# A decode forward-and-backward kernel: ten resident weight chunks, 1 MB zero stores issued by GpSimd alone, and a VectorE share in the w1 backward

## The chip, the cores and the metric

The kernel runs on one core of one Trainium2 chip. The metric is the time of one execution on the device in microseconds (us). Most executions of one kernel agree within a few tenths of a per cent, but different chips differ by more, so every kernel is compared with runs of the kernel before on the same chip. Runs are labelled fast or slow by their time and their clock.

Engines in the profile: PE is TensorE, PEld its weight loads, DVE is VectorE, ACT is ScalarE, POOL is GpSimd, SP is SyncE. A trailing q (SPq, POOLq) is the engine's instruction queue. "L138" is a line of the kernel. GB/s is what the 16 DMA engines moved.

## The reference, cut to what matters

One token (1,024 numbers) goes through attention A, an MLP B, the same A again and the same B again, each with a layer norm and a residual. Then all gradients are formed.

```python
    # D = 1024, 32 heads of 128, 4 groups of keys and values, F = 3584, Sk = 32768, W = 4096
    def _A_ref(x, k_cache, v_cache, wq, wo):
        q = (x @ wq).reshape(...)
        k = jnp.repeat(k_cache[:, :, Sk - W:, :], rep, axis=1)   # only the last 4,096 keys
        v = jnp.repeat(v_cache[:, :, Sk - W:, :], rep, axis=1)
        ...
        return softmax(q k * Dh ** -0.5) v @ wo
    def _B_ref(x, w1, b1, w2):
        h = x @ w1 + b1
        return mish(h) @ w2
    x = x + _A_ref(_layernorm(x), k_cache, v_cache, wq, wo)      # A1
    x = x + _B_ref(_layernorm(x), w1, b1, w2)                    # B2
    x = x + _A_ref(_layernorm(x), k_cache, v_cache, wq, wo)      # A3
    x = x + _B_ref(_layernorm(x), w1, b1, w2)                    # B4
    # outputs: x and the gradients of x, k_cache, v_cache, wq, wo, w1, b1, w2
```

The gradients of k_cache and v_cache have the shape of the whole caches. Outside the window of 4,096 keys they are zero, and these zeros have to be written: 2 caches x 4 groups x 28,672 x 128 numbers of 2 bytes, 58.7 MB. That is a third of all bytes this kernel moves. The zeros depend on nothing, so they can be stored at any time: they are the filling with which the DMA can be kept busy while TensorE works through a chain.

## The kernel before

The order of the stages is A1, B2, A3 and B4 forward (B4 fused with its backward), then A3 backward, the w2 pass and the w1 backward of B2, A1 backward, and last the "end": outer products of columns and rows, which are the weight gradients, copied from PSUM to SBUF and stored. The weight wo is cut in 16 chunks of 0.5 MB; nine stay resident in SBUF (`NR = 9`), the others go through six stream buffers (`NB = 6`) each time they are needed, as do w1 and w2.

The zeros come from a tile of 4 KB per partition, in 112 stores of 0.5 MB. GpSimd issues 76 of them in the background, behind a copy (`gate_t`) that waits for a value of the stage; SyncE issues the remaining 36 in A1 backward, as soon as its last weight loads are out.

```python
    ZC = 2048
    zt = keep.tile([P, ZC], BF16, name="zt")
    nc.gpsimd.memset(zt[:], 0.0)
    # ... cut: zero_jobs is the list of 112 pieces [P, ZC] of the two outputs
    def zeros(n):
        for _ in range(min(n, len(zero_jobs))):
            nc.sync.dma_start(zero_jobs.pop(0), zt[:])
    gate_t = keep.tile([P, 1], BF16, name="gate_t")
    def bg_zeros(n, after):
        if n:
            nc.gpsimd.tensor_copy(gate_t[:], after[:, 0:1])
        for _ in range(min(n, len(zero_jobs))):
            nc.gpsimd.dma_start(zero_jobs.pop(0), zt[:])
    # ... cut
    Z = dict(B2=3, A3=16, B4=[5, 2, 1, 2, 1, 2, 6], A3c=6, A3d=26, W1=3, A1c=3, A1d=36)
```

Z says how many stores each stage issues: B2, A3 and B4 forward, A3c and A3d in A3 backward, W1 in the w1 backward, A1c and A1d in A1 backward.

The w1 backward streams 16 half rows of w1. T loads one and transposes its 14 blocks of 128x128 (the matvec here needs w1 with the other axis on the partitions); M multiplies a half row with the gradient of the hidden layer.

```python
        def T(i):
            w = w1_load(i)
            ws[i] = w
            xpose(*alt_blocks(w[:, 0:1024], 4))
            xpose(*alt_blocks(w[:, 1024:1792], 3))
        def M(i, _):
            w, t, hf = ws.pop(i), i // 2, i % 2
            for b in range(NW2):
                fb = hf * NW2 + b
                mv(nacc, t, w[:, b * P:(b + 1) * P], sv["dh_bf"][:, fb:fb + 1], i == 0 and b == 0, fb == TF - 1)
        level()
        bg_zeros(Z["W1"], sv["dh_bf"])
        pipe(list(range(2 * TD)), T, M)
        return ln_bwd(nacc.cols(0, TD), sv["n32"], sv["rstd"], g_col, lname, nxt)
```

## Time and profile before

The kernel takes 451.71 us (median of 3 runs, 450.68 to 451.8). The profiled execution took 456.97 us and is labelled slow.

From the page of the kernel before: the span, the busy share of the DMA engines (tenths, 40 equal slices of 11.4 us), what they moved, the packets, and the queue that GpSimd fills.

```profile
span 454.9 us, 11941 instructions
DMA  8999997999999978999999799999999999999994
GB/s 323 385 412 422 407 409 281 381 322 370 417 416 384 404 238 282 354 392 411 419 413 414 273 362 349 321 400 417 415 417 420 418 416 417 419 418 419 419 420 172
DMA packets 52257, 172.25 MB, mean 379 GB/s; under 512 B 5200, under 2 KB 12396, under 8 KB 51180
q0 software_dynamic: 11040, 39.86, 22.0%
```

Where nothing holds the DMA back it moves 415 to 420 GB/s. At 418 GB/s the 172.25 MB take 412 us, so only 43 us of the span are DMA time not used. This gives a measure for each stage, called "lost": the stage's length minus its bytes divided by 418 GB/s. From about 300 us to the end almost nothing is lost: there the kernel is bound by DMA. The dips lie earlier.

The TensorE timeline of the kernel before shows the waits that the change aims at (start, busy us, instruction, and in brackets the idle time before it and what ended it):

```profile
140.31 0.56 PE L229 MATMUL sm<-o_pair,wo_c 128*128 128x16 bf16 x16 [3.62 <-DMA wo_c<-in_A_wo_dram]
162.84 0.60 PE L229 MATMUL sm<-nB_pair,w_b 128*128 128x16 bf16 x16 [4.50 <-DMA w_b<-in_B_w_dram]
210.23 1.03 PE L193 MATMUL tps<-ident_bf,wo_c 128*128 128x128 bf16 x8 [2.65 <-DMA wo_c<-in_A_wo_dram]
```

The seventh chunk of wo has to wait until one of six buffers is free.

### The profile page before, as it was taken

The page shows a single profiled execution, that of the slowest core. Times are in us where ns is not written, and L with a number is a line of the kernel's source. Part 1 is how long each engine was busy: PE and PEld are TensorE (multiplying, and loading weights), DVE is VectorE, ACT ScalarE, POOL GpSimd, SP SyncE. Part 2 cuts the span into 40 slices and gives each one's busy share as a digit, 9 for nine tenths or more (in the row PEclk, how much of TensorE's full clock was granted, in tenths as well). Part 3 has the DMA queues.
Part 4 walks back from the last instruction along what each step waited for, and adds up shares of the span by engine and source line. Part 5 has one row for each costly group of instructions (what it writes and reads, how often), then busy time and mean ns, then how long its engine had stood idle before and what let it go on. Part 6 is the DMA issues. An engine that isn't in the chain of part 4 may idle for free.

```text
span 454.9 us, 11941 instructions
## 1 busy us (share of the span) xinstructions
PE 324.7 (71%) x5107; PEld 224.4 (49%) x5107; DVE 236.6 (52%) x489; ACT 225.2 (50%) x262; POOL 56.6 (12%) x146
## 2 busy tenths in 40 slices
PE   0566854497896968985999888977868679897300
PEld 0334524387566968974687888844631111121000
DVE  3124101197422736683344874572359889999400
ACT  1122100075332837777365553536329899989400
POOL 2000000001422111341242002042010000000000
PEclk9997565578967969997879557999975555555555
DMA  8999997999999978999999799999999999999994
GB/s 323 385 412 422 407 409 281 381 322 370 417 416 384 404 238 282 354 392 411 419 413 414 273 362 349 321 400 417 415 417 420 418 416 417 419 418 419 419 420 172
DMA packets 52257, 172.25 MB, mean 379 GB/s; under 512 B 5200, under 2 KB 12396, under 8 KB 51180
## 3 DMA queue, kind: packets, MB, share of 16 engines
q1 hardware_dynamic: 41120, 131.61, 74.5%
q0 software_dynamic: 11040, 39.86, 22.0%
q8 instruction: 40, 0.66, 0.5%
q14 instruction: 13, 0.11, 0.1%
q10 hardware_dynamic: 44, 0.01, 0.0%
HBM read 72.89 MB, written 98.58 MB: 377 GB/s over the span
## 4 chain that ended last, share of the span: by engine, by line
PE 21%; ACT 12%; DMA 7%; issue 4%; SPq 3%; DVE 3%; DVEq 0%; POOL 0%; ACTq 0%; POOLq 0%
PE ops L229 7%; PE tps L193 7%; ACT wq_b L148 6%; DMA w_c<-in_B_w_dram 4%; PE acc L229 3%; SPq L129 3%; DMA wo_c<-in_A_wo_dram 2%; ACT st_o L148 2%; DMA out_dram<-zt 1%; ACT wo_b L148 1%; ACT K L148 1%; ACT V L148 1%; PE d L229 1%; PE tps L623 1%; ACT wo_c L148 1%
## 5 line engine op out<-in xcount | busy, mean ns | idle before, releaser
L138 POOL DMA_DIRECT2D out_dram<-zt x76 | 40.4, 536 | 44.5 <-DMA out_dram<-zt 41.9
L229 PEld LDWEIGHTS <-w_c 128*128 128x128 bf16 x1120 | 37.3, 103 | 16.7 <-DMA w_c<-in_B_w_dram 13.4
L633 ACT COPY w_c<-tps 128x1024 bf16<-128x1024 bf16 x28 | 28.2, 1012 | 21.7 <-PE tps L623 11.8
L229 PE MATMUL ops<-V 2*128 2x512 bf16 (+1 forms) x160 | 34.8, 598 | 5.9 <-ACT wq_b L148 3.4
L647 DVE CUSTOM_DVE_ANT_0 scr<-w_c,gbc 128x1024 bf16<-128x1024 bf16 x28 | 34.2, 1220 | 4.3 <-DMA w_c<-in_B_w_dram 2.2
L145 DVE CAST wq_b<-ops 128x1024 bf16<-128x1024 f32 (+1 forms) x31 | 33.8, 1148 | 3.8 <-PE ops L229 3.2
L148 ACT CAST wq_b<-ops 128x1024 bf16<-128x1024 f32 (+1 forms) x33 | 33.7, 1140 | 2.2 <-PE ops L229 2.0
L148 ACT COPY K<-tps 128x1024 bf16<-128x1024 bf16 x19 | 18.7, 1029 | 30.2 <-PE tps L193 30.2
L229 PE MATMUL ops<-wo_b 2*128 2x512 bf16 x120 | 23.3, 567 | 10.9 <-ACT wq_b L148 7.2
L229 PEld LDWEIGHTS <-V 128*128 128x128 bf16 (+2 forms) x416 | 14.2, 102 | 27.8 <-issue 27.6
L623 PE MATMUL tps<-ident_bf,w_c 128*128 128x128 bf16 x224 | 24.5, 276 | 1.1 <-DMA w_c<-in_B_w_dram 0.7
L148 ACT COPY w_b<-tps 128x1024 bf16<-128x1024 bf16 x20 | 19.5, 1015 | 6.7 <-PE tps L193 6.7
L145 DVE COPY K<-tps 128x1024 bf16<-128x1024 bf16 x13 | 8.9, 690 | 25.8 <-PE tps L193 25.8
L193 PE MATMUL tps<-ident_bf,K 128*128 128x128 bf16 x256 | 22.1, 252 | 0.1
L229 PE MATMUL q<-wq_b,nA_pair 128*32 128x512 bf16 x128 | 11.2, 440 | 15.0 <-DMA wq_b<-in_A_wq_dram 14.9
L193 PEld LDWEIGHTS <-K 128*128 128x128 bf16 x256 | 18.6, 115 | 4.5 <-issue 4.4
L813 DVE CUSTOM_DVE_ANT_0 wo_c<-wo_c,gbc 128x1024 bf16<-128x1024 bf16 x14 | 16.4, 1217 | 8.0 <-DMA wo_c<-in_A_wo_dram 4.3
L229 PEld LDWEIGHTS <-wo_b 2*128 2x128 bf16 (+1 forms) x152 | 5.6, 99 | 29.3 <-issue 28.6
L623 PEld LDWEIGHTS <-w_c 128*128 128x128 bf16 x224 | 18.5, 124 | 1.7 <-issue 0.9
L148 ACT CAST K<-ops 128x1024 bf16<-128x1024 f32 x18 | 17.7, 1014 | 2.5 <-PE ops L229 1.8
L193 PE MATMUL tps<-ident_bf,w_c 128*128 128x128 bf16 x224 | 17.1, 236 | 2.3 <-DMA w_c<-in_B_w_dram 2.3
L193 PE MATMUL tps<-ident_bf,wq_b 128*128 128x128 bf16 x256 | 18.0, 238 | 1.0 <-issue 1.0
(323 smaller groups left out, 651.9 us busy)
## 6 DMA issues: line engine op xcount, KB each, us to landing
out_dram<-zt POOLq DMA_DIRECT2D x76, 512.0 KB, 10.6
out_dram<-zt SPq DMA_DIRECT2D x36, 512.0 KB, 10.3
wo_c<-in_A_wo_dram SPq DMA_DIRECT2D x28, 512.0 KB, 8.4
w_c<-in_B_w_dram SPq DMA_DIRECT2D x32, 448.0 KB, 6.4
w_c<-in_B_w_dram SPq DMA_DIRECT2D x28, 512.0 KB, 6.0
out_dram<-wq_b SPq DMA_DIRECT2D x17, 512.0 KB, 11.4
wq_b<-in_A_wq_dram SPq DMA_DIRECT2D x16, 512.0 KB, 11.6
out_dram<-K SPq DMA_DIRECT2D x8, 1024.0 KB, 12.7
```

The source lines that it names most:

```text
L129: nc.sync.dma_start(zero_jobs.pop(0), zt[:])
L138: nc.gpsimd.dma_start(zero_jobs.pop(0), zt[:])
L145: nc.vector.tensor_copy(out_ap, in_ap)
L148: nc.scalar.copy(out_ap, in_ap)
L193: nc.tensor.transpose(ps[:, b, :], ap, ident_bf[:])
L229: nc.tensor.matmul(out_ap, lhsT=lhsT, rhs=rhs, start=start, stop=stop, skip_group_check=True, **kw)
L623: nc.tensor.transpose(self.ps[c][:, b, :], w[:, 1, b * P:(b + 1) * P], ident_bf[:])
L633: nc.scalar.copy(self.w[c][:, 1, :], self.ps.pop(c)[:].rearrange("p b c -> p (b c)"))
L647: nc.vector.tensor_tensor_reduce(out=scr[:], in0=w[:, 0, :], in1=gbc[:], scale=1.0, scalar=0.0, op0=ALU.mult, op1=ALU.add, accum_out=self. ...
L813: nc.vector.tensor_tensor_reduce(out=w[:, 0, :], in0=w[:, 0, :], in1=gbc[:], scale=1.0, scalar=0.0, op0=ALU.mult, op1=ALU.add, accum_out=w ...
```

## The change

Its intent: keep a tenth chunk of wo in SBUF, so that six late chunks meet six buffers; find the room for it by shrinking constants and by halving the tile of zeros (2 KB per partition, read four times for a store of 1 MB, with half as many instructions); let GpSimd issue all zeros and place them anew; and in the w1 backward let VectorE sum 1,024 of every 3,584 columns, with the matvecs two tiles behind the transposes. Small parts: warm-up matmuls in three gaps, a broadcast moved behind the first loads of B2, a row layout by four small matmuls.

```diff
-NR = 9
+NR = 10
...
-    ZC = 2048
-    zt = keep.tile([P, ZC], BF16, name="zt")
+    ZC = 4096
+    zt = keep.tile([P, ZC // 4], BF16, name="zt")
     nc.gpsimd.memset(zt[:], 0.0)
+    zt2 = zt[:, None, :].to_broadcast([P, 4, ZC // 4])
...
-    def zeros(n):
-        for _ in range(min(n, len(zero_jobs))):
-            nc.sync.dma_start(zero_jobs.pop(0), zt[:])
+                zero_jobs.append(zflat[:, i * ZC:(i + 1) * ZC].rearrange("p (a b) -> p a b", a=4))
...
-        if n:
+        if n and after is not None:
             nc.gpsimd.tensor_copy(gate_t[:], after[:, 0:1])
         for _ in range(min(n, len(zero_jobs))):
-            nc.gpsimd.dma_start(zero_jobs.pop(0), zt[:])
+            nc.gpsimd.dma_start(zero_jobs.pop(0), zt2)
... (mlp_fwd, B2)
-        gbc = bcast_row(g_bf)
+            if i == 4:
+                gbc = bcast_row(g_bf)
+                bg_zeros(Z["B2a"], n_bf)
... (w1 backward)
+        def V(i):
+            if i % 2 == 0:
+                wv = ws[i][:, 0:1024].rearrange("p (y t) -> p t y", t=2)
+                nc.vector.tensor_tensor_reduce(out=wv, in0=wv, in1=big[0][:].rearrange("p (t y) -> p t y", t=2), scale=1.0, scalar=0.0,
+                                               op0=ALU.mult, op1=ALU.add, accum_out=tw[:, i // 2:i // 2 + 1])
...
-        pipe(list(range(2 * TD)), T, M)
+        V(0)
+        for i in range(2, 2 * TD):
+            T(i)
+            V(i)
+            M(i - 2)
+        M(2 * TD - 2)
+        M(2 * TD - 1)
... (A1 backward)
             after_stream()
-            zeros(Z["A1d"])
...
             nextprep(2)
+            bg_zeros(Z["A1d"], None)
             warm(3)
...
             rows_put(area["Rq"], 1, "dq", "heads")
+            bg_zeros(Z["A1e"], None)
...
-    Z = dict(B2=3, A3=16, B4=[5, 2, 1, 2, 1, 2, 6], A3c=6, A3d=26, W1=3, A1c=3, A1d=36)
+    Z = dict(B2a=1, B2={NW2 - 2: 1}, A3=6, B4=[0, 1, 1, 1, 1, 1, 2], A3c=3, A3d=15, B4w={}, W1=0, A1c=6, A1d=5, A1e=100)
... (cut: onesD as a broadcast of one column, pat removed, row_layout and over_groups by tile_position, warm-up matmuls, order of late chunks)
```

In the new Z a unit is 1 MB. The last 12 stores (A1e) are issued by GpSimd behind `rows_put(... "dq" ...)`, a few copies on GpSimd that need the result of the attention backward (dq).

More of the change, by code (lines that the diff above doesn't have):

```diff
@@ L98 @@
     nc.scalar.dma_start(b_row, B_b1.rearrange("(c x) -> c x", x=2 * P))
-    onesD = keep.tile([P, P], FP32, name="onesD")
-    nc.vector.memset(onesD[:], invD)
+    ones1 = keep.tile([P, 1], FP32, name="ones1")
+    nc.vector.memset(ones1[:], invD)
+    onesD = ones1[:, 0:1].to_broadcast([P, P])
     eps_t = keep.tile([P, 1], FP32, name="eps_t")
@@ L124 @@
             for i in range(per // ZC):
-                zero_jobs.append(zflat[:, i * ZC:(i + 1) * ZC])
-    def zeros(n):
-        for _ in range(min(n, len(zero_jobs))):
-            nc.sync.dma_start(zero_jobs.pop(0), zt[:])
+                zero_jobs.append(zflat[:, i * ZC:(i + 1) * ZC].rearrange("p (a b) -> p a b", a=4))
     gate_t = keep.tile([P, 1], BF16, name="gate_t")
     def bg_zeros(n, after):
-        if n:
+        if n and after is not None:
             nc.gpsimd.tensor_copy(gate_t[:], after[:, 0:1])
         for _ in range(min(n, len(zero_jobs))):
-            nc.gpsimd.dma_start(zero_jobs.pop(0), zt[:])
+            nc.gpsimd.dma_start(zero_jobs.pop(0), zt2)
     ev = [0.0, 0.0]
@@ L261, in __call__, with over_groups @@
             return self.ap[:, j:j + 5:4]
+    def over_groups(out, rhs, start, stop):
+        for c in range(NC):
+            mm(out[32 * c:32 * c + 32, :], fold[:], rhs, start, stop, tile_position=(0, 32 * c))
     pre = []
@@ L281, in ln_fwd @@
         sps = sm_tile(P, 2 * TD)
-        nc.tensor.matmul(sps[:], lhsT=onesD[:], rhs=xx[:], start=True, stop=True)
+        nc.tensor.matmul(sps[:], lhsT=onesD, rhs=xx[:], start=True, stop=True)
         if name == "A3":
@@ L298, in ln_fwd, with ln_bwd @@
         return n32, n_bf, rstd
-    def ln_bwd(dn_ps, n32, rstd, g_col, name, nxt):
+    def ln_bwd(dn_ps, n32, rstd, g_col, name, nxt, more=None):
         tt = work.tile([P, 2 * TD], FP32, name="tt")
-        nc.vector.tensor_copy(tt[:, 0:TD], dn_ps)
+        if more is None:
+            nc.vector.tensor_copy(tt[:, 0:TD], dn_ps)
+        else:
+            nc.vector.tensor_add(tt[:, 0:TD], dn_ps, more)
         nc.vector.tensor_mul(tt[:, TD:], tt[:, 0:TD], n32[:])
         sps = sm_tile(P, 2 * TD)
-        nc.tensor.matmul(sps[:], lhsT=onesD[:], rhs=tt[:], start=True, stop=True)
+        nc.tensor.matmul(sps[:], lhsT=onesD, rhs=tt[:], start=True, stop=True)
         if nxt == "A1":
@@ L391, in row_layout @@
         x = area[name].rearrange("p (g d) -> p g d", g=G)
-        ps = psum1([P, P], BF16, "rps")
-        nc.tensor.transpose(ps[:, 0:P], col32[:], ident_bf[:])
+        ps = psum1([P, P], FP32, "rps")
+        for c in range(NC):
+            mm(ps[32 * c:32 * c + 32, 0:P], col32[:], ident_bf[:], True, True, tile_position=(0, 32 * c))
         for g in range(G):
@@ L404, in pad_cols @@
                              src_ps.rearrange("p (g h) -> p g h", g=G), ACT.Copy, scale=sc)
-        rep = keep.tile([P, NC, HQ], BF16, name=name + "_rep")
+        rep = keep.tile([P, HQ], BF16, name=name + "_rep")
         nc.vector.tensor_copy(
-            rep[:].rearrange("p c (g h) -> p c g h", g=G),
-            pad[:].rearrange("p (g x) -> p g x", x=40)[:, None, :, 0:8].to_broadcast([P, NC, G, 8]))
+            rep[:].rearrange("p (g h) -> p g h", g=G), pad[:].rearrange("p (g x) -> p g x", x=40)[:, :, 0:8])
         return rep
@@ L506, in attn_fwd @@
         sdg = work.tile([P, HQ], FP32, name="sdg", tag="u")
-        nc.vector.tensor_scalar(out=sdg[:, 0:32], in0=pat[:, 0, :], scalar1=ssum[:, 0:1], scalar2=None, op0=ALU.mult)
+        nc.vector.tensor_scalar(out=sdg[:, 0:32], in0=fold[:], scalar1=ssum[:, 0:1], scalar2=None, op0=ALU.mult)
         sps = sm_tile(P, HQ)
-        nc.tensor.matmul(sps[:, 0:32], lhsT=onesD[:], rhs=sdg[:, 0:32], start=True, stop=True)
+        nc.tensor.matmul(sps[:, 0:32], lhsT=onesD, rhs=sdg[:, 0:32], start=True, stop=True)
         rbc = work.tile([P, HQ], FP32, name="rbc", tag="r")
@@ L528, in attn_fwd @@
         lps = sm_tile(P, 1)
-        nc.tensor.matmul(lps[:], lhsT=pat[:].rearrange("p c x -> p (c x)"), rhs=ssum[:], start=True, stop=True)
+        over_groups(lps, ssum[:], True, True)
         lns = work.tile([P, 1], FP32, name="lns")
@@ L540, in attn_fwd @@
         late, early = list(range(NR, NO)), list(range(NR))
-        order = early + late if first else late[0:1] + early + late[1:]
+        order = early + late if first else late[0:3] + early + late[3:]
         for i, c in enumerate(order):
@@ L554, in attn_fwd @@
                 rows_sel2(yr, Cols8(yacc.cols(0, TD), False))
-            if not first and i == 0:
-                held[NO - 1] = wo_load(NO - 1)
             if not first:
@@ L650, in rest @@
                     self.bwd(c - 1, g_bf)
-                if c == NW2 - 2 and zn:
-                    bg_zeros(zn, self.wg[:, c, :])
+                if c in zn:
+                    bg_zeros(zn[c], self.wg[:, c, :])
             self.bwd(NW2 - 1, g_bf)
@@ L774, in mlp_bwd_w1, with blocks @@
         ws = {}
+        tw = work.tile([P, TD], FP32, name="tw", tag="xx", padded_shape=[P, 2 * TD])
+        big = []
+        def blocks(i):
+            return range(8 if i % 2 == 0 else 0, NW2)
         def T(i):
@@ L778, in T, with M @@
             ws[i] = w
-            xpose(*alt_blocks(w[:, 0:1024], 4))
+            if i % 2:
+                xpose(*alt_blocks(w[:, 0:1024], 4))
             xpose(*alt_blocks(w[:, 1024:1792], 3))
-        def M(i, _):
+        def M(i):
             w, t, hf = ws.pop(i), i // 2, i % 2
-            for b in range(NW2):
+            for b in blocks(i):
                 fb = hf * NW2 + b
-                mv(nacc, t, w[:, b * P:(b + 1) * P], sv["dh_bf"][:, fb:fb + 1], i == 0 and b == 0, fb == TF - 1)
+                mv(nacc, t, w[:, b * P:(b + 1) * P], sv["dh_bf"][:, fb:fb + 1], i == 0 and b == 8, fb == TF - 1)
+        def V(i):
+            if i % 2 == 0:
+                ev[0] += 1.3
+                wv = ws[i][:, 0:1024].rearrange("p (y t) -> p t y", t=2)
+                nc.vector.tensor_tensor_reduce(out=wv, in0=wv, in1=big[0][:].rearrange("p (t y) -> p t y", t=2), scale=1.0, scalar=0.0,
+                                               op0=ALU.mult, op1=ALU.add, accum_out=tw[:, i // 2:i // 2 + 1])
         level()
         bg_zeros(Z["W1"], sv["dh_bf"])
-        pipe(list(range(2 * TD)), T, M)
-        return ln_bwd(nacc.cols(0, TD), sv["n32"], sv["rstd"], g_col, lname, nxt)
+        rep8 = work.tile([P, TD, P], BF16, name="rep8", tag="kp")
+        nc.vector.tensor_copy(rep8[:], sv["dh_bf"][:, 0:TD, None].to_broadcast([P, TD, P]))
+        T(0)
+        T(1)
+        top("two")
+        big.append(pools["top"].tile([P, D], FP32, name="dhbc"))
+        for k in range(TD):
+            at = (k % 2) * 4 + k // 2
+            mm(big[0][:, at * P:(at + 1) * P], rep8[:, k, :], ident_bf[:], k < 2, True)
+        V(0)
[5 more added lines that the diff above has]
+        M(2 * TD - 1)
+        return ln_bwd(nacc.cols(0, TD), sv["n32"], sv["rstd"], g_col, lname, nxt, tw[:])
     def attn_bwd(g_col, g_bf, lname, sv, first, nxt):
@@ L829, in attn_bwd @@
         T(0)
-        bwd_rows2(dacc, wo_kept[NR - 1], NR - 1, g_bf, started=False)
+        for c in range(8, NR):
+            bwd_rows2(dacc, wo_kept[c], c, g_bf, started=c > 8)
         T(1)
@@ L845, in attn_bwd @@
                 lambda: rows_put(area["R1"], 1, "dh", "pieces"),
-                lambda: row_layout(sA3["dorep"][:].rearrange("p c x -> p (c x)"), "do3"),
-                lambda: row_layout(sA3["qrep"][:].rearrange("p c x -> p (c x)"), "q3"),
+                lambda: row_layout(sA3["dorep"], "do3"),
+                lambda: row_layout(sA3["qrep"], "q3"),
             ])
@@ L898, in attn_bwd @@
                 lambda: rows_put(area["Rq"], 0, "nA", "rep"),
-                lambda: row_layout(sA1["dorep"][:].rearrange("p c x -> p (c x)"), "do1"),
-                lambda: row_layout(sA1["qrep"][:].rearrange("p c x -> p (c x)"), "q1"),
+                lambda: row_layout(sA1["dorep"], "do1"),
+                lambda: row_layout(sA1["qrep"], "q1"),
                 db1_out,
@@ L912, in attn_bwd @@
         for hf in range(2):
-            nc.tensor.matmul(lps[:], lhsT=pat[:].rearrange("p c x -> p (c x)"), rhs=sdp[:, hf:hf + 1], start=hf == 0, stop=hf == 1)
+            over_groups(lps, sdp[:, hf:hf + 1], hf == 0, hf == 1)
         sd = work.tile([P, 1], FP32, name="sd")
@@ L957, in col_out @@
     def col_out(cols, n, out_flat):
-        ps = psum1([2 * HQ, P], BF16, "rw")
+        ps = psum1([HQ, P], BF16, "rw")
         nc.tensor.transpose(ps[0:n, 0:P], cols, ident_bf[:])
-        rt = work.tile([2 * HQ, P], BF16, name="rt", tag="rt")
+        rt = work.tile([HQ, P], BF16, name="rt", tag="rw5", padded_shape=[HQ, 2 * P])
         nc.vector.tensor_copy(rt[0:n, :], ps[0:n, 0:P])
@@ L1131, in nextprep @@
             prep.pop(0)()
-    Z = dict(B2=3, A3=16, B4=[5, 2, 1, 2, 1, 2, 6], A3c=6, A3d=26, W1=3, A1c=3, A1d=36)
+    Z = dict(B2a=1, B2={NW2 - 2: 1}, A3=6, B4=[0, 1, 1, 1, 1, 1, 2], A3c=3, A3d=15, B4w={}, W1=0, A1c=6, A1d=5, A1e=100)
     x1 = None
     gcolb = pair_col("gB", "B4", TD)
-    pat = keep.tile([P, NC, 32], FP32, name="pat")
     gmask = keep.tile([P, G], FP32, name="gmask")
@@ L1144 @@
     gcol = keep.tile([P, TD], FP32, name="gcol")
-    fold16f = work.tile([HQ, NO], FP32, name="fold16f")
+    fold16f = work.tile([HQ, NO], FP32, name="fold16f", tag="tt", padded_shape=[HQ, 2 * TD])
     def constants():
         nc.vector.reduce_sum(fold[:], ident_f[:].rearrange("p (c x) -> p x c", c=NC), axis=AX.X)
-        nc.vector.tensor_copy(pat[:], fold[:, None, :].to_broadcast([P, NC, 32]))
         nc.vector.reduce_sum(gmask[:], fold[:].rearrange("p (g h) -> p g h", g=G), axis=AX.X)
@@ L1183, in w2_ahead, with copy_gap, sel_gap, ln_gap @@
             w2p.tc(c)
-    hooks.update(copy=lambda: w2p.tp(0), sel=lambda: w2_ahead([0]), ln=lambda: w2_ahead([1, 2]))
+    def copy_gap():
+        w2p.tp(0)
+        warm(3)
+    def sel_gap():
+        w2_ahead([0])
+        warm(2)
+    def ln_gap():
+        w2_ahead([1])
+        warm(4)
+    hooks.update(copy=copy_gap, sel=sel_gap, ln=ln_gap)
     g2, g2b = attn_bwd(g3, g3b, "A3", sA3, True, "B2")
-    x4, wg2 = w2p.rest(3, g2b, x3, "x_B4", bcast_row(g2b), 0)
+    x4, wg2 = w2p.rest(2, g2b, x3, "x_B4", bcast_row(g2b), Z["B4w"])
     dh_of(wg2, "B2", sB2)
@@ L1219 @@
     dw_wide(lambda: area["Rq"], 512, 2048, False, out_4)
-    run(6)
-    while jobs:
-        zeros(1)
-        run(9)
-    zeros(1000)
+    run(1000)
+    bg_zeros(1000, None)
     assert not zero_jobs
```

## The prediction

> **What bounds it now.** The queue summary: 172.25 MB in a 454.9 us span. Where DMA is saturated the slice table reads 415 to 420 GB/s, and from 297 us to the end (A1 backward, all gradient stores) it stays there: that part is DMA-bound. At 418 GB/s the bytes need 412 us, so only 43 us of the span is unused DMA time: about 10 at launch and drain, the rest in dips (slices at 68-80, 91-113, 159-204, 250-296 us, 240 to 390 GB/s). In the dips TensorE's in-order chain is the limit, often waiting for one late load. So a change helps if it moves fewer bytes, or fills or shortens the dips.
>
> **The change, costed.**
> 1. Tenth resident wo chunk: late chunks drop from seven to six, the number of stream buffers. wo_c loads 28 to 24, resident 9 to 10: 3 x 0.52 MB less, -3.8 us of DMA. More important, the seventh chunk no longer waits for a buffer. The TensorE timeline shows that as stalls of 3.6 us (137-140), 2.65 us (208-210, after which the granted clock halves and eight transposes take 1.0 us instead of 0.61) and, through buffers it holds, 4.5 us on w_b at 158. I expect 8 to 10 us of these.
> 2. w1 backward (272.3 to 296.5, 24 us): 14 transposes take 0.80 us, 14 matvecs 0.34 us, two tiles 2.28 us. After: 20 and 20, 1.63 us: 13 us instead of 18 for all. VectorE adds eight sums of about 1.22 us (the same operation on w2), 10 us, which fits. Its 1.5 MB of zeros go too. The lag of two holds one more buffer, so loads are tight: stage 17 to 19 us, saving 6.
> 3. B2 forward: the broadcast (1.8 us wait at 69-71) leaves the start and 1 MB of zeros fills part of the hole: -2 us. Warm-up matmuls before the B2 w2 pass: -1 us.
> 4. Zeros: 76+36 stores of 0.5 MB become 56 of 1 MB, all on GpSimd. Before A1 backward they sum to 34.6 MB instead of 38.8, so 4 MB (10 us) move into the DMA-bound end: part of the shortening before 296 us is given back there.
> 5. The zero source is now 2 KB rows read four times. Rows of 3.5 KB store about 0.5% slower than 4 KB (416-417 against 419 GB/s in the slices). Estimated from that: 2 KB rows 2-4% slower on 58.7 MB, +3 to 5 us. The Trainium skill (DMA: Bandwidth & Descriptors, Queues, rings and completion order) says engines take turns between rings by packet; shorter zero packets would then favour the loads beside them. No run shows that yet.
>
> **Sum.** DMA idle 43 to about 33 us, bytes -3.8, descriptors +3: 11 us less. Predicted 441.5 us, 8 in 10 between 434 and 450. Chances: faster by over 2% 0.55, within 2% 0.43, slower 0.02.
>
> **What would show it.** w1 backward under 19 us; no TensorE wait over 2 us on wo_c in A3; A1 backward starting 15 to 20 us earlier, the end only 11 earlier; the end still over 410 GB/s; 170.7 MB in total; 14,000 more packets if the 2 KB rows become single packets.
>
> **What would make it wrong.** 2 KB zero packets much dearer than 4%; zeros of A3 backward (18.9 MB against 16.8) running into the w2 pass; GpSimd stuck behind its stores (it stalled 36 times already), so that its copies in A1 backward delay TensorE; zeros drained early, leaving staging too slow for the DMA.

## More of the kernel before

The window view of the kernel before gives this by stage. Columns: start and end, length, busy us (and count) of each engine, the granted TensorE clock, the DMA share, GB/s. The five stretches are A3 forward, B4, the w1 backward, A1 backward, and the end.

```profile
core 0: us, PE busy (x) PEld busy (x) DVE busy (x) ACT busy (x) POOL busy (x), PEclk, DMA share, GB/s
112.50:142.70 30.20, 24.25 (x431) 16.12 (x431) 9.03 (x27) 8.03 (x15) 8.64 (x17) 0.86 1.02 411
142.70:198.20 55.50, 47.86 (x1003) 47.25 (x1003) 33.19 (x126) 38.05 (x47) 13.33 (x31) 0.89 0.93 328
272.60:299.40 26.80, 23.25 (x459) 21.58 (x460) 13.98 (x27) 11.60 (x14) 3.13 (x8) 0.90 0.94 340
299.40:338.40 39.00, 29.62 (x516) 19.85 (x520) 18.58 (x56) 16.67 (x21) 10.11 (x45) 0.97 1.03 415
338.40:454.90 116.50, 69.05 (x376) 13.98 (x376) 81.99 (x73) 81.38 (x83) 0.52 (x1) 0.50 0.97 394
```

A1 backward moves 415 GB/s while TensorE works on its chain: the 36 stores of SyncE fill it.

The DMA issues of the kernel before (KB each, median us from issue to landing), and the timeline of SyncE's queue in A1 backward:

```profile
out_dram<-zt POOLq DMA_DIRECT2D x76, 512.0 KB, 10.6
out_dram<-zt SPq DMA_DIRECT2D x36, 512.0 KB, 10.3
```

```profile
302.40 43.27 SPq L129 DMA_DIRECT2D out_dram<-zt  x36
```

SyncE starts its 36 stores at 302.4 us and is busy issuing them for 43 us. Nothing else that it has to do in that time is needed sooner.

## The result, and the profile after

The changed kernel takes 475.35 us (474.33 to 476.19, 4 runs), the kernel before in the same rounds 451.75 us (450.68 to 453.37, 4 runs). The ratio is 1.0518, with a 95% interval of 1.048 to 1.0556. Here and below, a ratio is the mean time of one kernel's fast runs over that of the other's of the same rounds, so not quite the ratio of the medians that are quoted. The change makes the kernel 5% slower, where a gain of 2% had been predicted.

From the page of the kernel after (474.33 us, a fast run; the same lines as of before):

```profile
span 472.5 us, 11733 instructions
DMA  8999999999976999999999899997499999999997
GB/s 323 393 412 415 407 404 344 407 329 375 401 248 230 356 390 366 306 399 417 384 377 373 302 304 328 363 368 278 157 377 389 390 393 399 399 408 404 407 405 316
DMA packets 50927, 170.65 MB, mean 361 GB/s; under 512 B 4256, under 2 KB 11452, under 8 KB 49852
q0 software_dynamic: 15328, 58.74, 33.1%
```

Fewer bytes, and yet a longer span: 170.65 MB at 418 GB/s would be 408.3 us, so 64.2 us of DMA time are lost, against 43 before. Two things show at once in the GB/s line. There are new deep dips: slices 12 and 13 (248 and 230, where before had 416 and 384) and slices 28 and 29 (278 and 157, where before had 417 and 415). And the long tail, which stood at 415 to 420, now stands at 377 to 408.

The window view of the kernel after, by stage (A3 forward, B4, the w2 pass, the w1 backward, A1 backward, the end; columns as before):

```profile
core 0: us, PE busy (x) PEld busy (x) DVE busy (x) ACT busy (x) POOL busy (x), PEclk, DMA share, GB/s
113.70:143.30 29.60, 25.84 (x436) 16.08 (x436) 9.01 (x27) 8.03 (x15) 4.65 (x7) 0.80 0.90 334
143.30:193.40 50.10, 45.83 (x1004) 44.91 (x1005) 33.17 (x126) 37.73 (x47) 8.41 (x17) 0.93 0.91 330
242.50:267.40 24.90, 17.02 (x408) 15.93 (x408) 17.89 (x33) 12.14 (x12) 0.00 (x0) 0.79 0.99 358
267.40:295.50 28.10, 20.32 (x339) 17.26 (x340) 17.11 (x34) 13.71 (x16) 2.24 (x5) 0.83 0.88 309
295.50:340.70 45.20, 34.07 (x537) 23.64 (x535) 18.62 (x54) 16.06 (x20) 20.46 (x59) 0.76 0.79 289
340.70:472.50 131.80, 69.41 (x376) 14.36 (x376) 81.94 (x73) 81.22 (x83) 4.77 (x7) 0.50 1.00 389
```

Lost DMA time by stage, in us, worked out from such windows (before, in its slow profile / after): A3 forward 0.5 / 5.9; B4 11.9 / 10.5; A3 backward 0.5 / 3.8; w2 pass 5.4 / 3.6; w1 backward 5.0 / 7.3; A1 backward 0.3 / 13.9; the end 6.7 / 9.1. A1 backward is the largest term. For B4 the slow profile makes the kernel before look worse than it is: in b_late (section 3), which is the kernel before up to A1 backward and has a fast profile, B4 loses only 7.6, so the change made it worse too. The DMA view of the kernel after from 316 to 342 us, in 40 slices of 0.65 us, shows what happens there:

```profile
DMA  9999999999999999863000000000000029999998
GB/s 353 403 384 372 397 359 397 403 366 384 372 397 378 384 372 378 309 252 126 19 0 0 0 0 0 0 0 0 0 0 11 0 88 397 391 328 321 284 391 302
```

For about 8 us, from 328 to 337 us, the DMA does nothing at all, with 12 MB of zeros still to store. In the same stretch the kernel before had "9" in all forty slices. The timeline of GpSimd in the kernel after says why:

```profile
334.89 0.53 POOL L1247 DMA_DIRECT2D out_dram<-wo_b  x1 [12.61 <-DVE wo_b L1246]
335.42 0.65 POOL L1022 COPY wo_b<-dq_pair 128x16 bf16<-128x16 bf16 x4
335.96 6.71 POOL L136 DMA_DIRECT2D out_dram<-zt  x9
```

GpSimd sat 12.6 us waiting for a value of VectorE (L1246, for the small store of the gradient of b1 at L1247), then made its copies of dq, and only then issued the zeros that come behind them in its program. It was not dq that it waited for. TensorE multiplies with dq 9 us before GpSimd copies it:

```profile
326.48 1.47 PE L227 MATMUL acc<-wq_b,dq_pair 128*32 128x512 bf16 x12 [0.29 <-ACT dq_pair L970]
```

The five stores placed earlier (A1d) were used up at 328 us. The zeros themselves waited for nothing; their issuer did.

Three waits from the TensorE timeline of the kernel after:

```profile
80.84 0.54 PE L227 MATMUL acc<-nB_pair,w_c 128*128 128x16 bf16 x14 [3.68 <-DMA w_c<-in_B_w_dram]
252.93 0.59 PE L227 MATMUL acc<-a_pair,w_c 128*128 128x16 bf16 x16 [4.91 <-DMA w_c<-in_B_w_dram]
288.83 1.21 PE L191 MATMUL tps<-ident_bf,w_c 128*128 128x128 bf16 x14 [1.74 <-DMA w_c<-in_B_w_dram]
```

The first is in B2, where a 1 MB store of zeros now shares the DMA with the first loads of w1; the second is in the w2 pass, beside the zeros of A3 backward; the third is one of eight such waits in the w1 backward.

### The profile page after: what moved, and what is told of

The parts are those of the page before. It is cut to its first block, busy times and chain, and to the rows that moved or that the text cites. A ratio compares the mean times of both kernels' runs of the same rounds, so it can differ in the third digit from the quotient of the medians.

```text
span 472.5 us, 11733 instructions
## 1 busy us (share of the span) xinstructions
PE 321.7 (68%) x5060; PEld 216.8 (46%) x5060; DVE 237.3 (50%) x491; ACT 227.1 (48%) x264; POOL 57.8 (12%) x125
## 2 busy tenths in 40 slices
DMA packets 50927, 170.65 MB, mean 361 GB/s; under 512 B 4256, under 2 KB 11452, under 8 KB 49852
## 3 DMA queue, kind: packets, MB, share of 16 engines
q0 software_dynamic: 15328, 58.74, 33.1%
## 4 chain that ended last, share of the span: by engine, by line
PE 21%; ACT 15%; DMA 8%; issue 5%; DVE 2%; SPq 1%; POOL 1%; DVEq 0%; ACTq 0%; POOLq 0%
PE ops L227 6%; PE tps L191 5%; DMA w_c<-in_B_w_dram 5%; ACT wq_b L146 5%; PE acc L227 3%; DMA out_dram<-K 3%; ACT K L146 3%; ACT wo_b L146 2%; ACT V L146 2%; ACT st_o L146 1%; PE wps L152 1%; PE sm L227 1%; ACT wo_c L146 1%; PE tps L626 1%; PE rw L1009 1%
## 5 line engine op out<-in xcount | busy, mean ns | idle before, releaser
L227 PEld LDWEIGHTS <-w_c 128*128 128x128 bf16 x1056 | 34.7, 102 | 26.0 <-DMA w_c<-in_B_w_dram 20.0
L146 ACT COPY K<-tps 128x1024 bf16<-128x1024 bf16 x20 | 19.5, 1024 | 29.1 <-PE tps L191 29.0
L143 DVE CAST wq_b<-ops 128x1024 bf16<-128x1024 f32 (+1 forms) x29 | 31.6, 1151 | 3.5 <-PE ops L227 2.8
L146 ACT CAST wq_b<-ops 128x1024 bf16<-128x1024 f32 (+1 forms) x31 | 31.7, 1136 | 2.2 <-PE ops L227 2.0
L143 DVE CAST K<-ops 128x1024 bf16<-128x1024 f32 x14 | 16.6, 1222 | 14.6 <-DMA out_dram<-K 13.5
L626 PE MATMUL tps<-ident_bf,w_c 128*128 128x128 bf16 x224 | 21.9, 257 | 0.7 <-DMA w_c<-in_B_w_dram 0.7
L227 PE MATMUL acc<-a_pair,w_c 128*128 128x16 bf16 x448 | 15.6, 172 | 7.9 <-DMA w_c<-in_B_w_dram 7.8
L191 PE MATMUL tps<-ident_bf,K 128*128 128x128 bf16 x256 | 19.3, 234 | 0.0
L146 ACT COPY w_c<-tps 128x1024 bf16<-128x1024 bf16 (+1 forms) x16 | 13.7, 909 | 11.4 <-PE tps L191 11.3
L191 PEld LDWEIGHTS <-K 128*128 128x128 bf16 x256 | 16.3, 105 | 3.1 <-issue 3.0
L146 ACT COPY wq_b<-tps 128x1024 bf16<-128x1024 bf16 x16 | 15.2, 1046 | 5.0 <-PE tps L191 4.9
```

The lines of the kernel that those rows point to most:

```text
L143: nc.vector.tensor_copy(out_ap, in_ap)
L146: nc.scalar.copy(out_ap, in_ap)
L191: nc.tensor.transpose(ps[:, b, :], ap, ident_bf[:])
L227: nc.tensor.matmul(out_ap, lhsT=lhsT, rhs=rhs, start=start, stop=stop, skip_group_check=True, **kw)
L626: nc.tensor.transpose(self.ps[c][:, b, :], w[:, 1, b * P:(b + 1) * P], ident_bf[:])
```

## The experiments

The theories. **Holes**: zeros are issued too late or are missing where the DMA has nothing else (A1 backward first, then A3 and B4). **Rows**: stores from 2 KB rows are slower. **Addresses**: the new layout of SBUF moves the start of tiles, and stores from these addresses are slower. The addresses in the built program (start within a partition, remainder by 256 bytes; they come from the build, not from the profile) are:

```
                 zt    wq_b   wo_b   K, V   stream buffers
before            0     32     32      0      224
after            32     64     64     32      192
a_ztalign         0     64     64     32      192
a_align           0      0      0      0      192
b_shift32        32     64     64     32      224
b_2k_shift32     32     64     64     32      224
```

**Loads**: the new w1 backward is not faster, because it is held up by its loads. All kernels gave correct results.

### 1. Rows and addresses, in the kernel before

b_again is the kernel before, unchanged, for a profile. b_2k reads the zeros from 2 KB rows. b_shift32 allocates 32 bytes ahead of the tile of zeros. b_2k_shift32 does both.

```diff
# b_2k
+    zt2 = zt[:, None, 0:ZC // 2].to_broadcast([P, 2, ZC // 2])
-                zero_jobs.append(zflat[:, i * ZC:(i + 1) * ZC])
+                zero_jobs.append(zflat[:, i * ZC:(i + 1) * ZC].rearrange("p (a b) -> p a b", a=2))
-            nc.sync.dma_start(zero_jobs.pop(0), zt[:])      # and in bg_zeros
+            nc.sync.dma_start(zero_jobs.pop(0), zt2)
# b_shift32 (b_2k_shift32: both)
+    pair_col("nA", "A1", TD)        # 32 bytes per partition, ahead of zt
     ZC = 2048
     zt = keep.tile([P, ZC], BF16, name="zt")
```

> Control: the kernel before, unchanged, profiled again beside the others. If the slower gradient stores of the changed kernel (403-407 GB/s at the end against 419-420) come from the chip or the run, this profile will read about 405 too; if from the program, it reads 419-420. The zero stores alone in attention A3 forward should again read about 418 GB/s.

> The kernel before with only the source of the zero stores cut to 2 KB rows, each read twice; sizes, queues, times of issue and all addresses as before. Theory R (short source rows slow the zero stores): the stretch where zeros run alone (112-137 us) falls from 418 to about 380 GB/s and the whole kernel takes 10 to 15 us more. Theory A (start addresses) and theory S (where the zeros are placed): no change within 2 us.

> The kernel before with one 32-byte tile allocated ahead of the zero tile, so that the zero tile, wq_b, wo_b, K and V start at the offsets modulo 256 bytes which they have in the changed kernel (32, 64, 64, 32, 32 instead of 0, 32, 32, 0, 0). Nothing else differs. Theory A: the gradient stores at the end fall from 419 to about 405 GB/s and the zeros fall below 418; 4 to 10 us more. Theories R and S: no change within 2 us.

> Both edits on the kernel before: 2 KB source rows and all tiles 32 bytes later, so the zero tile starts 32 bytes past a multiple of 256. Each alone left the total within 0.5% (zeros 413-414 and 412-414 GB/s). Theory RA (it takes both): zeros alone fall to about 383 GB/s as in the changed kernel, and 8 to 12 us are lost, about 462 us. If the two only add: zeros about 410, within 3 us of 452.

Measured: b_again 455.91 us, one run of unknown state, beside 452.09 for the kernel before. b_2k 454.12 us, ratio 1.0033 (0.9981 to 1.0084), the same. b_shift32 452.19 us, ratio 0.9976 (0.9927 to 1.0025), the same. b_2k_shift32 458.9 us (kernel before in its call 452.75), ratio 1.014 (1.0074 to 1.0207): by the limit of 2% unclear, but its interval lies above 1. Neither part alone costs anything that can be told from nothing; together they cost 1.4%. Window views of A3 forward, where GpSimd's zeros fill the DMA (118 to 133 us), of b_again, b_2k, b_shift32 and b_2k_shift32 in turn; the last column is GB/s:

```profile
118.00:133.00 15.00, 13.40 (x274) 10.09 (x274) 7.04 (x19) 7.32 (x13) 5.18 (x10) 0.83 1.03 415
```

```profile
118.00:133.00 15.00, 13.40 (x286) 9.90 (x278) 6.91 (x19) 6.26 (x11) 7.94 (x11) 0.92 1.03 415
```

```profile
118.00:133.00 15.00, 13.40 (x280) 9.71 (x274) 7.04 (x19) 6.96 (x13) 4.93 (x10) 0.91 1.02 415
```

```profile
118.00:133.00 15.00, 12.75 (x266) 9.41 (x259) 7.03 (x19) 7.45 (x13) 7.40 (x11) 0.89 1.02 396
```

So in this stretch 2 KB rows are as fast as 4 KB rows where they start on a multiple of 256 bytes, 4 KB rows do not mind starting 32 bytes later, and 2 KB rows that start 32 bytes later lose 5% (415 to 396). In A1 backward, where SyncE issues the zeros, the four read 417 (b_again), 404 (b_2k), 412 (b_shift32) and 391 (b_2k_shift32) GB/s between 310 and 336 us, when the zeros of all four are under way: here short rows alone cost 3%, the shift alone 1% and both 6%.

The Trainium skill (DMA: Bandwidth & Descriptors, How a descriptor splits into AXI transactions) says that a transaction has to start from a 256-byte-aligned address and that a descriptor which starts elsewhere fetches bytes that it does not use. That agrees in direction with the loss of the misaligned short rows. What it does not tell is the interaction: a loss of 5% for 2 KB rows that start late, and none or 1% for 4 KB rows. The mechanism behind that stays open.

### 2. Addresses, in the kernel after

a_ztalign allocates the tile of zeros first. a_align allocates wq_b, wo_b, K and V first as well (these are also the staging buffers of the gradient stores at the end).

```diff
# a_ztalign (a_align: the last three lines too)
+    ZC = 4096
+    zt = keep.tile([P, ZC // 4], BF16, name="zt")
+    wq_b = keep.tile([P, TD, 2, J // 2], BF16, name="wq_b")
+    wo_b = keep.tile([P, NR, 2, D], BF16, name="wo_b")
+    kv_at = {nm: keep.tile([P, G, TK, DH], BF16, name=nm) for nm in ("K", "V")}
     x0 = keep.tile([P, TD], FP32, name="x0")
```

> The changed kernel with the zero tile allocated before x0, so that it starts at a multiple of 256 bytes (it started at 32 past one); its rows stay 2 KB, nothing else moves. Theory A: the zeros alone rise from about 378 towards 410 GB/s and the kernel loses 5 to 12 us of its 475. Theory R: still about 380 GB/s, time within 2 us of 475. Theory S: as R.

> The changed kernel with the zero tile, wq_b, wo_b, K and V all allocated first, so each starts at a multiple of 256 bytes. Against the version with the zero tile alone aligned (466.6 us) the gradient stores should return from 405 to 418 GB/s, as 64 bytes past 256 cost that in the shifted kernel before: about 3 us less, 463 us. If it is not the start address, stores stay at 405 and time at 466.

Measured: a_ztalign 466.6 us, ratio 1.0281 (1.0224 to 1.0339), slower than the kernel before, but by 2.4 points less than the kernel after (1.0518). a_align 467.72 us (463.9 to 471.09), ratio 1.0312 (1.0228 to 1.0396): no better than a_ztalign, the intervals overlap.

Window views of A3 backward (225 to 238 us, zeros from GpSimd), the kernel after first, then a_ztalign:

```profile
225.00:238.00 13.00, 13.00 (x232) 10.96 (x230) 7.96 (x12) 9.64 (x11) 2.27 (x3) 1.00 1.02 384
```

```profile
225.00:238.00 13.00, 13.00 (x227) 10.70 (x224) 7.10 (x12) 7.85 (x9) 1.51 (x2) 1.00 1.02 413
```

The zeros go from 384 to 413 GB/s by the address of one 2 KB tile. That profile is slow, but a_align and a_sp12, with the same start of zt, have fast ones and read 414 and 413 here. And a window of the gradient stores at the end (400 to 440 us), the kernel after first, then a_align:

```profile
400.00:440.00 40.00, 23.16 (x132) 5.20 (x131) 26.11 (x24) 24.68 (x27) 0.00 (x0) 0.50 1.02 403
```

```profile
400.00:440.00 40.00, 21.62 (x126) 4.77 (x119) 25.97 (x23) 24.36 (x26) 0.00 (x0) 0.50 1.03 419
```

In a_ztalign, with wq_b and wo_b 64 bytes late and K and V 32, this window reads 405; in b_again and b_2k (wq_b and wo_b 32 late, K and V 0) 418 and 419, in b_shift32 (64 and 32) 406. So the rate of the gradient stores follows the addresses of their sources as well. Which of these tiles costs is not shown, as in all these runs they move together. In the total this gain is not seen, neither between b_shift32 and the kernel before nor between a_ztalign and a_align. Why not is open. In the latter pair the hole in A1 backward may cover it, which is only argued.

### 3. The hole in A1 backward

a_sp12 is a_align with the last 12 stores issued by SyncE, in the place where the kernel before had its 36. a_sp12_only is the same in the kernel after, with its own addresses. b_late is the reverse, in the kernel before: SyncE issues 16 of its 36 stores, and GpSimd the other 20 behind its copies of dq.

```diff
# a_sp12, a_sp12_only
             after_stream()
+            for _ in range(12):
+                nc.sync.dma_start(zero_jobs.pop(0), zt2)
# b_late
             after_stream()
-            zeros(Z["A1d"])
+            zeros(16)
...
             rows_put(area["Rq"], 1, "dq", "heads")
+            for _ in range(20):
+                nc.gpsimd.dma_start(zero_jobs.pop(0), zt[:])
```

> As the aligned changed kernel, and the twelve zero stores that stood behind the dq columns on GpSimd are issued by SyncE when the wo chunks of A1 backward are through, as the kernel before did with its 36. Theory S (the rest of the loss is DMA left idle because zeros come too late): the 13.9 us of unused DMA in A1 backward fall under 3, and the time falls by 8 to 12 us, to about 453. If the zeros' place does not matter: no change from the aligned version.

> The changed kernel with its own addresses (zero tile 32 bytes past 256), and only the twelve last zero stores moved to SyncE in A1 backward. If the two causes add: 475 less about 11, 464 us, unused DMA in A1 backward mostly gone but the rate there still about 380-385 GB/s. If they are one cause: about 456 as with the addresses mended, or no gain at all.

> The kernel before with 20 of the 36 zero stores which SyncE issues in A1 backward moved to GpSimd behind its copies of the dq columns, where the changed kernel has its last twelve. Theory S: DMA idles some 8 to 12 us in A1 backward and the time grows by as much, to 460-464 us, at full rates of 415-419 GB/s elsewhere. If lateness alone costs nothing: within 2 us of 452.

Measured: a_sp12 456.04 us, ratio 1.0111 (1.0027 to 1.0195). a_sp12_only 461.99 us (458.53 to 464.56), ratio 1.0225 (1.0143 to 1.0308). b_late 461.38 us (458.01 to 463.97), ratio 1.0223 (1.015 to 1.0296). By the limit of 2% the last two are unclear; both intervals lie clearly above 1 and below the 1.048 of the kernel after.

The window of A1 backward in a_sp12, and in b_late:

```profile
290.40:334.10 43.70, 30.59 (x540) 20.17 (x544) 18.31 (x54) 15.95 (x20) 16.65 (x53) 0.88 1.02 401
```

```profile
294.80:333.80 39.00, 29.63 (x512) 19.85 (x512) 18.60 (x56) 16.67 (x21) 14.49 (x54) 0.97 0.81 326
```

The DMA view of b_late, 316 to 336 us in 40 slices of half a microsecond:

```profile
DMA  9999999999996320000010000000199899999999
```

The theory of the hole holds in both directions. With the 12 stores moved back to SyncE, A1 backward goes from 289 to 401 GB/s, and the lost time there from 13.9 to 1.8 us; in the kernel's own addresses (a_sp12_only) the lost time goes to 3.3 us and 2.9% is won (1.0518 to 1.0225), about 13 us. With 20 half-size stores moved behind GpSimd's copies, and nothing else touched, the kernel before gets the same hole (a loss of 8.6 us in A1 backward where it had 0.3) and becomes 2.2% slower, 9.8 us by the medians. Its GpSimd stands in the same line: 10.0 us for the small store of the gradient of b1, while dq is ready 5 us before that store goes out. How much would be won by moving only this small store out of the way was not run.

The Trainium skill (DMA: Bandwidth & Descriptors, Issuing engines are not separate DMA queues) says that all issuers feed the same 16 DMA engines, and that several issuers only save the time of issuing. The runs do not contradict it, but they add what matters here: an issuer is an in-order queue, and a store that needs nothing inherits every wait that stands before it. Issuing is not what costs (0.75 us a store); waiting in line is (12.6 us).

### 4. The other holes

a_sp12_z is a_sp12 with more zeros in A3 and B4 forward, taken out of A3 backward. a_fill takes no zeros at the start of B2, more in A3 forward and at the end of B4, and leaves A3 backward nearly as it was; SyncE issues 11.

```diff
# the kernel after (and a_sp12)
     Z = dict(B2a=1, B2={NW2 - 2: 1}, A3=6, B4=[0, 1, 1, 1, 1, 1, 2], A3c=3, A3d=15, ...)
# a_sp12_z
     Z = dict(B2a=1, B2={NW2 - 2: 1}, A3=8, B4=[2, 1, 1, 1, 1, 1, 3], A3c=3, A3d=10, ...)
# a_fill
     Z = dict(B2a=0, B2={NW2 - 2: 1}, A3=8, B4=[0, 1, 1, 1, 1, 1, 3], A3c=3, A3d=14, ...)
```

> As the run before it, and the earlier zeros moved back towards where the kernel before had them: A3 forward 8 instead of 6, B4 10 instead of 7, A3 backward 10 instead of 15. Theory S: unused DMA in A3 forward and B4 (5.9 and 10.5 us) falls to about 0.5 and 6, the wait of 4.9 us for a w2 tile at the start of the w2 pass goes: 5 to 8 us less, about 446, under the kernel before. If that idle time is not on the path: no change.

> The aligned changed kernel with eleven zero stores on SyncE in A1 backward, none at the start of B2, eight in A3 forward, eight in B4 with none in its first block, fourteen in A3 backward. Theory S (unused DMA time decides): A3 forward loses about 1 us of DMA instead of 5.8, B2 2 less, A3 backward and the w2 pass as in the version with 12 on SyncE; about 449 us, under the kernel before at 452. If it is above 454, the places of the zeros are not what is left.

Measured: a_sp12_z 456.62 us, ratio 1.0093 (1.0026 to 1.016), no gain over a_sp12. The hole of A3 forward did close (lost 5.8 to 0.8 us), but the five stores taken out of A3 backward were missing there and in the w2 pass (7.0 and 7.2 us lost): the hole only moved. a_fill 450.57 us (its kernel before 453.82), ratio 0.9938 (0.9859 to 1.0017): A3 forward lost 0.9 us, and B2 was 41 to 42 us long (a_fill, a_fill_lag1) instead of 45.2 (45.9 in a_sp12), without the 3.68 us wait for w1 that the zeros at its start had made; its longest wait there is 1.10 us.

### 5. The w1 backward by itself

b_w1 puts the new w1 backward (with the new argument of the layer norm's backward) into the kernel before, and nothing else. b_w1_lag1 has the matvecs one tile behind the transposes instead of two. a_fill_lag1 has that in a_fill. a_fill_w1z is a_fill_lag1 with three of SyncE's stores put into the w1 backward.

```diff
# b_w1_lag1 against b_w1, a_fill_lag1 against a_fill
         V(0)
+        M(0)
         for i in range(2, 2 * TD):
             T(i)
             V(i)
-            M(i - 2)
-        M(2 * TD - 2)
+            M(i - 1)
         M(2 * TD - 1)
# a_fill_w1z against a_fill_lag1: W1=3 instead of 0, and
-            for _ in range(11):
+            for _ in range(8):
                 nc.sync.dma_start(zero_jobs.pop(0), zt2)
```

> The kernel before with the new w1 backward alone (VectorE sums 1024 columns of every even tile, matvecs two tiles behind). Theory P (TensorE was the limit there, as predicted): the stage from the end of the w2 pass to the next broadcast falls from 27-29 to 21-23 us and the time by about 5 us, to 447. Theory L (six stream buffers and the landing time of a load set its pace): the stage stays at 27-29 us with more DMA waits on TensorE, the time within 2 us of 452.

> As the run before it, with the matvecs one tile behind the transposes, as the kernel before had them, so that a buffer is free one tile sooner. Theory L: one more load in flight, the stage shortens by 2 to 4 us against lag two. Theory P: lag does not matter, or TensorE waits for VectorE and the copies and the stage gets longer.

> As the run before it with lag one in the w1 backward. Theory L: its stage shortens from 27-28 to about 24-25 us and, as everything after it is limited by DMA, the time by as much, to about 446. Theory P: no gain.

> The best version so far (447.5 us, lag one) with three of the eleven SyncE zero stores moved to the start of the w1 backward. Theory F (free filler): the stage stays at 24 to 25 us between the two transposed sums, its unused DMA falls from 7.4 to about 2 us, and the time falls by 3 to 6 us to about 443. Theory L (the landing time of each load sets the pace, and 1 MB stores ahead of the loads lengthen it): the stage grows by 4 to 7 us and the time stays at 447 or rises.

Measured: b_w1 452.58 us, ratio 0.9986 (0.9935 to 1.0038). b_w1_lag1 452.1 us, ratio 0.9997 (0.9921 to 1.0072). Both are the same as the kernel before: the new stage by itself wins nothing. From its first transposes to the sum of the layer norm it takes 26.7 us in b_w1 and 26.6 in b_w1_lag1; the old stage takes 27.0 in b_late, where it is unchanged and the profile is fast. In the kernel after it takes 24.7 us, but without the 1.5 MB of zeros that the others have in it.

Why? TensorE has less to do (16.9 us busy in the 24.65 us of the stage, against 23.1 of 27.0 in b_late), but it waits for loads of w1 eight times, 6.9 us together (6.2 in b_w1), where the old stage waited 3.2 (b_late). The DMA is not full then: it moves 306 GB/s. The waits of SyncE's queue show what the loads wait for, in the kernel before (268 to 297 us) and in the kernel after (267 to 292 us); columns: the issuing line, what it waited for, total us, times, longest:

```profile
engine line waited for: us in total, times, longest us
SPq L359 <- PE acc L229: 14.0, 13, 2.2
...
SPq L359 <- DVE w_c L145: 2.7, 2, 2.5
```

```profile
engine line waited for: us in total, times, longest us
SPq L364 <- PE acc L227: 8.7, 7, 3.3
SPq L353 <- PE acc L227: 5.4, 3, 2.9
SPq L364 <- DVE tw L804: 4.2, 2, 3.8
```

L364 (before: L359) is the load of a half row of w1. It waits for a stream buffer, that is for the matvecs that read the buffer last ("PE acc"), and now also for the sum on VectorE ("DVE tw"). Six buffers go round: free, loaded (4 to 6 us from issue to landing), transposed, multiplied, free. 16 half rows in 24.65 us are 1.54 us each, 9.2 us for a turn of six. Taking 6 us of work from TensorE does not shorten the turn, since the landing stays and the lag of two keeps a buffer longer. That the turn of the buffers sets the pace is read from these waits; how much of a turn each part makes was not measured singly. It holds for the lag of two only. With lag one TensorE's waits for loads shrink, from 6.2 us in b_w1 to 3.7 in b_w1_lag1 and from 5.7 in a_fill to 2.2 in a_fill_lag1, yet the stage hardly does (26.7 to 26.6 us, 25.2 to 24.5): waits of the matvecs for ScalarE's copies of the transposed blocks come in their place, 3.0 and 3.1 us where there were 0.3. So loads are not the only limit of this stage.

With lag one in a_fill: 447.47 us (445.76 to 448.93), ratio 0.9867 (0.9813 to 0.9921) against 0.9938 for a_fill. The intervals overlap, so the lag by itself is worth at most a little, and in b_w1 it showed nothing. a_fill_w1z: 444.47 us (443.03 to 447.48), but its kernel before took 450.18 us on that chip, so the ratio is 0.9872 (0.9799 to 0.9946), the same as of a_fill_lag1. Its 3 MB of zeros lengthened the stage from 24.5 to 30.3 us: zeros beside loads that somebody waits for are not free.

**The best version** is a_fill_lag1: 1.3% faster than the kernel before. Its interval excludes 1. From its page:

```profile
GB/s 315 387 418 426 416 414 335 407 348 345 415 414 358 315 369 374 395 399 416 414 414 381 341 288 303 346 413 413 412 415 409 419 418 414 421 417 418 421 420 209
```

No slice is under 280 but the last, and the tail is at 409 to 421 again. Its span is 444.0 us, so 35.7 us are lost (444.0 - 170.65 MB / 418 GB/s), close to the 33 that the prediction had for the changed kernel.

## Why the prediction was wrong, point by point

In terms of the ratio to the kernel before, the experiments take the 5.2% apart like this (each percentage is against "after", or, where it says "more", against the row above):

| version | ratio | what it removes |
|---|---|---|
| after | 1.0518 | |
| a_sp12_only | 1.0225 | the last 12 zeros behind GpSimd's copies: 2.9% |
| a_ztalign | 1.0281 | 2 KB rows from a start 32 bytes off: 2.4% |
| a_sp12 | 1.0111 | both (and the other tiles aligned): 4.1% |
| a_fill | 0.9938 | too few zeros in A3, B4; zeros beside B2's first loads: 1.7% more |
| a_fill_lag1 | 0.9867 | lag one instead of two: 0.7% more, not told from nothing |

The first two causes sum to 5.3% singly and to 4.1% together. The intervals are too wide to tell whether they overlap.

- **"What bounds it now" was right**: DMA-bound from A1 backward on, and a change helps if it shortens the dips. It was not applied to the new dips that the change makes. "DMA idle 43 to about 33 us" is the term that failed: it became 64.2 us. The 43 was itself too high, as it came from the slow profile: a run of 451.5 us has a span of 449.4 us, which leaves about 37.
- **Step 4 ("Zeros") is the step that failed.** It counted how many bytes move to the end, and took for granted that the DMA has them at hand in the part that it called DMA-bound. It did not ask when the 12 stores called A1e are issued. The answer was in the program: behind copies of dq, and these behind the small store of the gradient of b1, on an engine that works in order and stood 12.6 us before that store. The cost is 13 us (a_sp12_only), and b_late makes the same hole in the kernel before. In its list of what could go wrong the prediction had "zeros drained early" and "GpSimd stuck behind its stores", but not that the stores are stuck behind GpSimd's other work. The fewer zeros in A3 and B4 forward (13 stores of 1 MB for what were 35 of 0.5 MB) were not costed either; A3 forward loses 5.9 us there, against 0.9 in b_late.
- **Step 5 ("The zero source") named the right suspect with the wrong size and the wrong cause.** 3 to 5 us were predicted; a_ztalign wins 2.4%, about 9 to 11 us. The estimate from rows of 3.5 KB does not carry over: 2 KB rows as such cost nothing to be seen in the total (b_2k), and 2 KB rows from a start 32 bytes off cost 5 to 7% of the rate. The new start came from the order of allocations, which the prediction did not look at. The 14,000 more packets did not come: packets fell from 52,257 to 50,927, and those of GpSimd's queue kept 3.6 to 3.8 KB each. The profile does not count rows as packets here. The prediction's point from the Trainium skill (DMA: Bandwidth & Descriptors, Queues, rings and completion order), that engines take turns by packet, was thus not put to the test, as the packets did not become shorter.
- **Step 1 (tenth chunk) was half right.** 170.65 MB came as predicted, and no TensorE wait over 2 us on wo_c is left in A3. A3 backward takes 49.1 us against 49.8 in b_late (fast, unchanged up to there), A3 forward 29.6 against 32.7. But the 8 to 10 us expected were read from a profile in the slow state. B4 took 55.5 us there, 49.6 in b_late and 50.1 after: the 4.5 us wait on w_b was mostly no loss of a fast run (1.9 us in b_late, 1.8 after), so little was to be had from it.
- **Step 2 (w1 backward "17 to 19 us, saving 6") failed.** 24.7 us, and by itself no gain (b_w1). The prediction summed engine times, noted that "loads are tight", and did not work out the turn of six buffers: TensorE's 13 us became 16.9 us of work and 6.9 us of waits for loads.
- **Step 3 (B2) had the wrong sign.** B2 takes 45.2 us after (43.4 to 45.9 in the fast runs with zeros at its start), 42.2 to 44.0 in the fast profiles with the old B2, and 41 to 42 us in a_fill and the runs built on it, without those zeros. Here, filling a hole with zeros delayed the loads that would have ended it.
- **"A1 backward starting 15 to 20 us earlier"**: it starts at 295.5 us, where b_late and b_2k have 294.8 and 295.5. Nothing was won before it. Of the gains in A3, part went into the w2 pass, with the 4.91 us wait on w2 beside the zeros of A3 backward (3.02 in b_late); that risk the prediction did name (24.9 us, 22.6 in b_late).
- **"The end still over 410 GB/s"**: 389, and 403 after the last zeros. The sources of the gradient stores start 32 and 64 bytes late (section 2).

What stays open: why short rows and a late start cost so much more together; what the tenth chunk, the moved broadcast, the warm-up matmuls and the row layout are worth singly, as none was run by itself; whether the faster gradient stores of a_align show in the total; what the lag is worth alone; and how the 7 to 8 us that B4 and the w1 backward each still lose in a_fill and a_fill_lag1 could be filled, as zeros in the w1 backward lengthened it (a_fill_w1z).

## What to carry to other kernels

Filler transfers are only as early as the queue that issues them: give them to an engine that has nothing to wait for in that stage, and check for every one of them what stands before it in program order. When the order of allocations changes, read off the start address of every tile that is a large DMA's source: here 32 bytes cost 7% of the rate of short rows, and a tile allocated first gave it back. In a ring of stream buffers, work out the buffer's turn (wait, landing, use, release) before counting on a gain from work taken off an engine: here 6 us less of TensorE's work won nothing; and a stall seen in one profile should be looked for in a fast profile before it is counted as a gain.

## What the Trainium skill lacked or had wrong

- DMA: Bandwidth & Descriptors, How a descriptor splits into AXI transactions: it tells that an unaligned start costs extra beats (units of transfer) and counts them for 96 and 576 B, but gives no rate for large stores. An estimate by its count, if each row is one descriptor: 65 beats instead of 64 for a 2 KB row that starts 32 bytes late, 1.6%, and half of that for a 4 KB row. Measured for stores from SBUF: 2 KB rows that start 32 bytes past a multiple of 256 ran at 384 GB/s, 413 when aligned, 7% less and so more than the count gives; 4 KB rows that start 32 bytes past ran at 412 to 415, 415 to 417 when aligned. For gradient stores, sources 64 (wq_b, wo_b) and 32 bytes past (K, V) gave 403 to 406, sources 32 and 0 past, or all at 0, 415 to 419.
- DMA: Bandwidth & Descriptors, Rules for kernel authors: 1 MiB or more per DMA for the highest bandwidth. Here stores of 0.5 MB in a full queue already ran at 415 to 419 GB/s, and the 1 MB stores of a_align (from 2 KB rows) at 414: the larger size gained no rate.
- DMA: Bandwidth & Descriptors, Issuing engines are not separate DMA queues: right as it stands, but it names only the time of issuing. Moving 20 stores of 0.5 MB behind dependent work in GpSimd's queue cost 9.8 us (b_late), by what stood ahead of them in the queue.
- No page that was used says how the profile's count of packets relates to rows: with rows of 2 KB read four times the packets of GpSimd's queue stayed at 3.8 KB each (58.74 MB in 15,328).
